# Emitting the first batch's attention steps inside a high-priority scheduling block

## The chip, the cores and the metric

The kernel runs on one core of one Trainium2 chip. The metric is device time in microseconds (us) of one execution; a timing is the median of several executions. The engines are PE (TensorE), DVE (VectorE), ACT (ScalarE), POOL (GpSimd) and SP (SyncE, which here only issues DMAs).

## What the kernel computes

All arithmetic is on float32 data. The inputs q, k, v have shape 8 x 8 x 576 x 64 (batch, heads, sequence, head width), p has 32 rows in place of 576.

```
p_packed = softmax(p k^T / 8) v            # 32 packed rows for each head
attn     = softmax(q p_packed^T / 8) p_packed
x = attn, heads side by side               # 4608 tokens x 512
h = x @ w_in                               # 512 -> 1024
s = h * softmax(h)
ln = (s - mean(s)) / sqrt(var(s) + 1e-6) * g_ln
y = ln @ w_out                             # 1024 -> 512
out = max(y @ w1, y @ w2, y @ w3) @ w_out2 # 512 -> 768 -> 512
```

The MoE weights arrive as float64 words, so w_in, w_out, w1, w2, w3 and w_out2 must be decoded to float32 on the chip before they are used.

## The kernel before

**The first part of the program** is attention plus the first expert block, in token tiles of 128 (36 tiles, `tok_hidden`). The attention of a batch is folded into w_in: the packed values of the batch, `ppT`, are multiplied with the decoded w_in, which gives `Mh` and `Ml` (a high and a low part). A tile's hidden row is then the product of its second-softmax weights `ah`, `al` with `Mh`, `Ml` (line 500, `h`). The second part (line 737 onward) is a Strassen-like product with w1, w2, w3 and the output product (line 984).

**A batch's attention** is a `Packed` object whose pieces are called by letters, each with a group or pair number: K `keys` (transposes of p and k into `pT` and `kT`, lines 312 and 319), S `scores` (line 328, then row maxima L336, L337 on DVE, exponentials L341 on ACT, reciprocals L346 to L349), E `weights` (transposes of the exponentials, L357), V `values` (L368, scaled on ACT at L377, transposed at L383 into `ppT`), M `product` (L395, then `Mh` L247 on ACT and `Ml` L248 on DVE), Q `queries` (transposes of q into `qT`, L412), X `tokens` (L428 on PE; then on DVE transposes L434, maximum L438, subtraction L439, sum L442, L443, reciprocal L444, product L445, transposes back L459; the exponential L440 and the cast to `ah`, L460, on ACT; `al`, L461, on POOL). Lower-case k, v, q are loads: one 576 KB DMA for a group of four heads of k or v (L291, L295), three DMAs of 288 KB together for a pair of heads of q (L304 twice, L307 once).

**Buffers that gate loads**: the two k tiles and the two v tiles of a batch share one tag with two buffers, the four q tiles share a tag with two buffers. A third load waits until a buffer is released by its last reader. The raw words of w_in (eight pieces of 512 KB, L179) have six buffers.

**The decode of w_in** runs beside the first batch's attention. A piece takes one or two ACT instructions (L116, L118), three or four DVE instructions (L121, L124, L127, for every second piece L129) and one or two POOL instructions (L132, or L134 and L135). Pieces are numbered by c = 0 to 3 (128 rows each) with two halves each. M0 needs c = 0 and 1, M1 needs c = 2 and 3. Decoding w_out (L199, L200 with the same helpers) follows.

**Order of the work.** The order on each engine's queue is not written by hand. A scheduler walks the program against modelled durations and gives an idle engine, DMA queue or buffer to the ready instruction with the smallest priority number. The number is the place in the program text: earlier text, smaller number. Waiting for another engine's result is then fixed into the queue: at run time each engine takes its queue in order. The list that orders the first batch is

```
st=['K0S0K1v0q0', '', 'v1', 'q1E0', 'S1V0Q0E1Q1V1M0', 'q2', 'q3Q2Q3X0X1M1', ''],
```

and the loop that emits it stands at the end of the set-up, after the loads of p, k and six pieces of w_in:

```
for i, step in enumerate(CFG['st']):
    first.run(step)
    for d in dec[:2]:
        d()
    dec = dec[2:]
    if i == 0:
        dec += [decode_w_in(NPAIR - 1, n) for n in range(2)]
```

So after each of the first four steps the decode of one c is emitted; the step that begins with S1 comes behind all of the decode in the text. After the loop come the loads of g_ln and w_out, the second batch's attention (`second`, in small steps called between the tiles) and the tiles themselves. Tile 0 needs K, S, E, V, Q, M of both groups and X0; X1 serves tiles 2 and on.

Of the kernel before, what the change touches and what calls it, by code (L numbers as in the profile page):

```python
# [53 lines left out]
def kernel(  # L54
# [127 lines left out]
    def decode_w_in(c, n):  # L182
        ns = slice(n * 512, (n + 1) * 512)
        raw = wide(words(w_in)[c * P:(c + 1) * P, ns, :])
        t = lt_p.tile([P, TB], F32, tag="lh", name="dt")
        t2 = lt_p.tile([P, TB], F32, tag="ll", name="dt2") if CFG['l0'][n] == 'g' else None
        return lambda: [f() for f in decode(w_in_sb[:, c, ns], raw, t, t2, ENG[CFG['d0'][2 * (c % 2) + n]])]
# [616 lines left out]
    first, second = Packed(0), Packed(1)  # L804
# [2 lines left out]
    first.load(1)  # L807
    dec += [decode_w_in(c, n) for c in (1, 2) for n in range(2)]
    for i, step in enumerate(CFG['st']):
        first.run(step)  # L810
        for d in dec[:2]:
            d()
        dec = dec[2:]
        if i == 0:
            dec += [decode_w_in(NPAIR - 1, n) for n in range(2)]
# [268 lines left out]
```

## Time and profile before

| | us |
|---|---|
| median of 3 timed executions | 1119.6 |
| lowest and highest of them | 1118.24 and 1119.76 |
| span of the profiled execution | 1119.7 |
| PE busy in it | 1061.3 (95%) |
| DVE, ACT, POOL busy | 735.0, 483.9, 273.9 |

The time of the profiled execution is its span; no other time of it is recorded, and it lies 0.1 us above the median of the timed runs. A row of the timeline view gives a start time in us from the span's start, a duration, the engine and the source line, the operation with its output and inputs, and in brackets how long the engine sat idle before it and which instruction ended the wait. SPq is the queue of DMA issues; a row of it is the issue, not the transfer. "x6" after a shape counts the instructions that were merged into the row.

### The profile page before, as it was taken

Reading aid. Unit: us, or ns where it says so; the run is one execution under the profiler, and the core shown is the slowest. Engines: PE = TensorE matmul, PEld = TensorE weight load, DVE = VectorE, ACT = ScalarE, POOL = GpSimd, SP = SyncE. Lnnn points to the kernel's source line nnn. Section 1 sums busy time; section 2 is a strip of 40 time slices with the busy share of each in tenths; the row PEclk is TensorE's granted clock in tenths of the full one; section 3 lists DMA queues with packets and bytes.
Section 4 is the critical chain, followed back from the end, with each engine's and each line's share of the span. In section 5 each row is a group of like instructions: output and inputs, shape, how many; then the busy total and the mean of one; then the engine's idle time right before and its main releaser. Section 6 shows DMA issues by size and latency. Waiting matters only on the chain.

```text
span 1119.7 us, 17559 instructions
## 1 busy us (share of the span) xinstructions
PE 1061.3 (95%) x6308; PEld 885.5 (79%) x6308; DVE 735.0 (66%) x1454; ACT 483.9 (43%) x951; POOL 273.9 (24%) x283
## 2 busy tenths in 40 slices
PE   4799999999999999999789999999999999999998
PEld 2456667676767777787678899989989999998996
DVE  5788897968787895766686734745664573572560
ACT  3676766665666666456343321321142131132112
POOL 3442311111112110103576410230041041132002
PEclk9798999999999999999899999999999999999999
DMA  9842636464565622310674533534454353443421
GB/s 260 195 104 58 183 106 178 128 167 125 134 177 139 167 83 63 113 38 19 225 226 141 175 119 121 169 112 133 144 167 132 114 177 117 121 123 104 132 76 57
DMA packets 132262, 149.01 MB, mean 133 GB/s; under 512 B 51536, under 2 KB 85328, under 8 KB 132176
## 3 DMA queue, kind: packets, MB, share of 16 engines
q1 hardware_dynamic: 132176, 147.89, 45.2%
q8 instruction: 50, 0.82, 0.3%
q14 instruction: 36, 0.29, 0.1%
HBM read 113.25 MB, written 34.60 MB: 132 GB/s over the span
## 4 chain that ended last, share of the span: by engine, by line
PE 52%; DVE 4%; issue 3%; POOL 2%; ACT 1%; DMA 1%; SPq 0%; DVEq 0%; POOLq 0%; ACTq 0%
PE m L737 31%; PE o L984 13%; PE y L591 4%; PE h L500 2%; POOL s L640 1%; PE tp L566 1%; DMA wt<-wdram 1%; DVE s L646 1%; DVE v L776 0%; POOL al L640 0%; DVE u L772 0%; PE mp L395 0%; DVE u L510 0%; DVE nm L506 0%; DVE r L759 0%
## 5 line engine op out<-in xcount | busy, mean ns | idle before, releaser
L591 PE MATMUL y<-lh,woh 128*128 128x512 f32 x288 | 118.5, 416 | 0.8 <-ACT lh L572 0.8
L772 DVE TENSOR_TENSOR u<-m,q 128x384 f32<-128x384 f32 x54 | 29.9, 554 | 134.7 <-ACT ob L993 75.7
L591 PE MATMUL y<-ll,woh 128*128 128x512 f32 x288 | 115.8, 402 | 0.0
L591 PE MATMUL y<-lh,wol 128*128 128x512 f32 x288 | 114.6, 398 | 0.0
L768 ACT COPY q<-m 128x384 f32<-128x384 f32 x54 | 25.9, 480 | 168.2 <-PE m L737 168.2
L799 POOL TENSOR_TENSOR hl<-cur,hh 128x384 fp32r<-128x384 f32 x36 | 37.7, 1047 | 243.8 <-ACT hh L798 243.8
L132 POOL TENSOR_TENSOR wt<-raw 128x256 f32<-128x256 f32 x56 | 34.4, 615 | 213.3 <-DVE raw L129 116.9
L984 PE MATMUL o<-w2h,hh 128*128 128x512 f32 x216 | 85.3, 395 | 0.0
L984 PE MATMUL o<-w2h,hl 128*128 128x512 f32 x216 | 85.3, 395 | 0.0
L984 PE MATMUL o<-w2l,hh 128*128 128x512 f32 x216 | 85.3, 395 | 0.0
L737 PE MATMUL m<-b22h,s 128*128 128x384 f32 x216 | 65.7, 344 | 2.3 <-DVE r L759 2.0
L591 PEld LDWEIGHTS y<-lh,woh 128*128 128x128 f32 x288 | 53.9, 189 | 14.2 <-ACT lh L572 1.1
L591 PEld LDWEIGHTS y<-lh,wol 128*128 128x128 f32 x288 | 54.6, 190 | 12.3
L737 PE MATMUL m<-t2h,s 128*128 128x384 f32 x216 | 64.2, 337 | 0.0
L591 PEld LDWEIGHTS y<-ll,woh 128*128 128x128 f32 x288 | 54.7, 190 | 11.7 <-issue 1.0
L737 PE MATMUL m<-t1h,s 128*128 128x384 f32 x216 | 63.7, 335 | 0.1
L737 PE MATMUL m<-t3h,s 128*128 128x384 f32 x216 | 63.5, 334 | 0.0
L798 ACT CAST hh<-cur 128x384 fp32r<-128x384 f32 x36 | 18.5, 514 | 90.4 <-DVE cur L785 49.0
L573 DVE SCALAR_TENSOR_TENSOR ll<-tp,g_sb,lh 128x512 fp32r<-128x512 f32 x72 | 52.0, 744 | 8.1 <-ACT lh L572 7.8
L572 ACT ACTIVATE lh<-tp,g_sb 128x512 fp32r<-128x512 f32 x72 | 47.3, 686 | 22.5 <-PE tp L566 22.4
L799 POOL TENSOR_TENSOR hl<-kept,hh 128x384 fp32r<-128x384 f32 x36 | 38.8, 1077 | 72.5 <-ACT hh L798 72.5
L506 DVE TENSOR_REDUCE nm<-h 128x1 f32<-128x1024 f32 x36 | 43.9, 1219 | 17.8 <-PE h L500 17.5
(189 smaller groups left out, 2912.2 us busy)
## 6 DMA issues: line engine op xcount, KB each, us to landing
s<-sdram SPq DMA_DIRECT2D x180, 256.0 KB, 2.8
kt<-in_k_dram SPq DMA_DIRECT2D x16, 576.0 KB, 5.2
vt<-in_v_dram SPq DMA_DIRECT2D x16, 576.0 KB, 4.8
ydram<-yt SPq DMA_DIRECT2D x36, 256.0 KB, 3.2
raw<-in_moe_w_dram SPq DMA_DIRECT2D x36, 256.0 KB, 2.9
b<-ydram SPq DMA_DIRECT2D x24, 384.0 KB, 3.5
sdram<-s SPq DMA_DIRECT2D x36, 256.0 KB, 2.1
out_dram<-ob SPq DMA_DIRECT2D x36, 256.0 KB, 2.0
```

What stands on the lines that cost most here:

```text
L132: add.tensor_tensor(out=dst, in0=f32(hi), in1=f32(lo), op=ALU.add)
L500: nc.tensor.matmul(h[:, n, :], lhsT=x, rhs=m[:, g, n * 512:(n + 1) * 512], start=(i == 0), stop=(i == len(ops) - 1),)
L506: nc.vector.tensor_reduce(out=nm, in_=hv, axis=AX.X, op=ALU.max, negate=True)
L572: last[nc.scalar] = nc.scalar.activation(lh, tp, AF.Copy, scale=gc)
L573: last[nc.vector] = nc.vector.scalar_tensor_tensor(out=ll, in0=tp, scalar=gc, in1=f32(lh), op0=ALU.mult, op1=ALU.subtract)
L591: nc.tensor.matmul(ys[half][m], lhsT=w[:, kc, ms], rhs=x, start=(kc == 0 and i == 0), stop=(kc == KFF - 1 and i == 2),)
L737: nc.tensor.matmul(out, lhsT=w, rhs=y, start=start and i == 0, stop=i == len(ops) - 1, skip_group_check=not start,)
L768: nc.scalar.copy(q, ba)
L772: add(out=u, in0=bb, in1=q, op=ALU.add)
L798: nc.scalar.copy(hh, t)
L799: nc.gpsimd.tensor_tensor(out=hl, in0=t, in1=f32(hh), op=ALU.subtract)
L984: nc.tensor.matmul(ops[i], lhsT=x[:, ts], rhs=w, start=(c == 0 and n == 0), stop=(c == KF2 - 1 and n == 2),)
```

## The change

The call that emits a step of the first batch's attention is wrapped in the scheduler's high-priority context. By its definition the context, when no offset is given, sets the priority counter to 0, the start of the program, and puts it back on exit. The instructions of each step, its DMA issues among them, are therefore numbered 0, 1, 2, ... anew in each of the eight steps, and everything emitted outside (the decode of w_in, the loads of p, k and w_in, the second batch, the tiles) is numbered as if the steps took no numbers. No instruction is added or removed and no buffer is changed.

```
     for i, step in enumerate(CFG['st']):
-        first.run(step)
+        with tc.high_priority():
+            first.run(step)
         for d in dec[:2]:
             d()
         dec = dec[2:]
```

## Rows read from the trace of the kernel before

**Rows 1.** The page, busy tenths of the span in 40 equal slices.
```profile
PE   4799999999999999999789999999999999999998
```

**Rows 2.** Windows: stretch, its length, busy us (instructions) of each engine, clock, DMA.
```profile
0.00:8.00 8.00, 0.67 (x3) 0.41 (x4) 0.00 (x0) 1.28 (x1) 1.69 (x15) 1.00 0.69 184
8.00:20.00 12.00, 10.15 (x63) 5.47 (x62) 8.57 (x15) 8.71 (x24) 3.67 (x3) 1.00 1.07 308
20.00:30.00 10.00, 0.88 (x48) 0.74 (x48) 8.76 (x18) 2.65 (x9) 5.95 (x5) 0.65 0.85 212
30.00:40.00 10.00, 8.86 (x88) 5.90 (x90) 6.09 (x11) 7.35 (x20) 5.69 (x5) 0.83 0.59 130
40.00:50.00 10.00, 5.95 (x37) 2.93 (x31) 9.12 (x18) 6.07 (x14) 4.02 (x3) 0.85 1.04 254
50.00:60.00 10.00, 9.80 (x46) 6.05 (x47) 6.58 (x13) 4.47 (x11) 3.87 (x3) 0.64 0.68 167
60.00:80.00 20.00, 17.57 (x188) 11.30 (x189) 16.98 (x43) 17.23 (x39) 10.51 (x8) 1.00 0.59 142
80.00:112.00 32.00, 29.90 (x153) 19.80 (x149) 26.08 (x60) 23.08 (x46) 6.44 (x11) 0.89 0.19 51
200.00:400.00 200.00, 197.07 (x1361) 142.91 (x1354) 163.45 (x411) 130.66 (x265) 31.37 (x47) 1.00 0.52 143
```

**Rows 3.** Timeline, all engines, 9 to 32 us.
```profile
9.51 0.43 DVE L121 TENSOR_SCALAR dt<-dt 128x512 int32<-128x512 int32 x1 [9.51 <-ACT dt L116]
...
21.58 0.45 DVE L336 TENSOR_REDUCE m<-s 128x1 f32<-128x288 f32 x1
...
28.19 0.20 DVE L337 TENSOR_SCALAR m<-m 128x1 f32<-128x1 f32 x1
28.49 0.50 ACT L341 ACTIVATE e<-s,m 128x288 f32<-128x288 f32 x1 [7.32 <-DVE m L337]
...
30.03 0.48 PE L383 MATMUL tp<-ident,ppz 128*128 128x128 f32 x1 [7.74 <-ACT ppz L377]
...
31.56 0.67 ACT L116 ACTIVATE dt<-raw 128x512 f32<-128x512 f32 x1
```

**Rows 4.** Timeline of the DMA issue queue, 10 to 36 us.
```profile
10.45 0.33 SPq L295 DMA_DIRECT2D vt<-in_v_dram  x1
10.82 2.80 SPq L304 DMA_DIRECT2D qtl<-in_q_dram  x2
...
31.69 0.92 SPq L304 DMA_DIRECT2D qtl<-in_q_dram  x2
```

**Rows 5.** DMA issues of 1.73 to 2.2 us (KB each, us from issue to landing).
```profile
kt<-in_k_dram SPq DMA_DIRECT2D x1, 576.0 KB, 6.0
```

**Rows 6.** DMA issues of 17.0 to 18.8 us and of 18.85 to 19.6 us.
```profile
raw<-in_moe_w_in_dram SPq DMA_DIRECT2D x1, 512.0 KB, 7.8
vt<-in_v_dram SPq DMA_DIRECT2D x1, 576.0 KB, 9.1
```

**Rows 7.** Timeline, all engines, 33 to 62 us.
```profile
33.85 0.88 PE L368 MATMUL pv<-vt,e1T 96*32 96x64 f32 x48
...
36.20 0.27 ACT L242 COPY ppT<-tp 128x128 f32<-128x128 f32 x1 [0.42 <-PE tp L383]
...
38.53 1.30 POOL L135 TENSOR_TENSOR w_in_sb<-raw,dt 128x512 f32<-128x512 f32 x1
...
39.59 2.16 PE L428 MATMUL st<-qT,ppT 128*64 128x256 f32 x16
...
41.58 1.89 PE L395 MATMUL mp<-w_in_sb,ppT 128*64 128x512 f32 x8
...
49.55 0.60 ACT L460 CAST ahsmall<-y 128x512 fp32r<-128x512 f32 x1
...
50.20 0.79 PE L500 MATMUL h<-Mh,ahsmall 128*128 128x512 f32 x1 [1.55 <-ACT ahsmall L460]
...
60.69 0.90 DVE L459 STREAM_TRANSPOSE y<-x 128x320 f32<-128x320 f32 x2
```

More of the change, by code (lines that the diff above doesn't have):

```diff
@@ L809 @@
     for i, step in enumerate(CFG['st']):
-        first.run(step)
+        with tc.high_priority():
+            first.run(step)
         for d in dec[:2]:
```

## The prediction

> **What bounds the kernel now.** I first read where PE is idle, since it is busy for 95% of the span. The slices of the page [rows 1] show the reader two thin places at the start and nearly full slices behind them but for a dip in the second half that this change does not touch. The windows [rows 2] give sizes: up to 60 us PE is busy 0.67 + 10.15 + 0.88 + 8.86 + 5.95 + 9.80 = 36.31 us, so idle for 23.7; from 60 to 112 it is idle for 4.5; from 200 to 400 it is 98.5% busy. What reaches PE earlier at the start therefore stays earlier to the end, and the start is where this change acts.
>
> In the start PE is not the limit; DVE is, and behind it the loads. DVE is busy for 39.12 us of the first 60 [rows 2]. Its idle time is 8.0 (0 to 8), 3.4 (8 to 20), 1.2 (20 to 30), 3.9 (30 to 40), 0.9 (40 to 50) and 3.4 (50 to 60). The first three are waits for loads at the beginning. The last three, 8.2 us together, come from one chain. DVE ends the second row maximum of S1 at 22.0, but the 0.20 us instruction that joins the two maxima stands behind decode work in the queue and runs only at 28.19; ACT waited 7.32 us for it, PE 7.74 us for what ACT does next [rows 3]. The next q load waits too: q2 is issued at 31.69 [rows 4] and q3 behind it, so X's products begin only at 39.59, and its cast on ACT ends at 49.55 + 0.60 = 50.15, when tile 0 starts at 50.20 [rows 7]. The last piece of w_in has the same fate: its words were issued by 18.8 and landed 7.8 us later [rows 6], near 26, but the decode of c = 3 begins on ACT at 31.56, behind the delayed exponentials [rows 3], and ends at 39.83 on POOL [rows 7].
>
> **The change, part by part.** *No work is added or taken away.* Instruction counts and sizes stay, so the whole sum is waits and order.
>
> *Attention before decode on DVE, ACT and PE.* The S1 step gets numbers from 0 instead of numbers behind all decode, so its small DVE instructions pass the decode. The decode of w_in is numbered from about 17 to 70 (seven instructions of set-up, ten loads, then 13 instructions for each c; counted in the text), and those of S1 (0 to 15) lie below all of it, those of X0 (17 to 35) below c = 2 and 3 and most of c = 1. V1 (66 and on) and M0 (94 and on) do not pass it. M0 also loses its place against the second batch's first transposes (81 to 98), which are short; I cost that at nothing, as PE has 23.7 us of room, and at the 2.2 us by which a run can be told from no change if that room is gone. What is to be had is the 8.2 us of DVE idle time in 30 to 60 us. The bounds are 0, if new waits replace the old, and 8.2 + 3.1 = 11.3, if the waits of 8 to 30 us (4.6, less the 1.5 us from 8 to DVE's first instruction at 9.51 [rows 3]) go as well. I take 8.2: those early waits are for loads, and the loads become no faster.
>
> *Loads.* Every DMA issue inside a step moves too. v1, q1, q2 and q3 are the first items of their steps, so they are numbered 0 to 2, ahead of p (7) and k0 (9). A free buffer goes to the smallest number that is ready; at the start all are free. So v1 takes one of the two k/v buffers, q1 and q2 the two q buffers, and all seven issues go out before p. That puts 576 + 2 x 288 = 1152 KB ahead of the first load that anything waits for. The price: between the landing of k0 (issued 1.74, 6.0 us, so 7.7) [rows 5] and that of v1 (18.91 + 9.1 = 28.0) [rows 6], 6112 KB came down: the eight pieces of w_in (4096 KB), k1, v0 and v1 (1728) and q0 (288). That is 301 KB per us, a full pipe, since both windows in it show DMA shares of 1.07 and 0.85 [rows 2]. So the moved loads cost 1152 / 301 = 3.8 us at the start of everything. The bounds are 0 (buffers given out in the order of the text after all) and 6.3 (the 184 GB/s of the first window [rows 2]); I take 3.8, from the full pipe.
>
> k1 loses its buffer to v1. It waits until K0 has read k0, then v0 waits for K1. I follow the bytes: k0 lands at 11.5; then c = 0, 1 and 2 (3072 KB), k1 (576), q3 (288), c = 3 (1024), q0 (288) and v0 (576), 5824 KB or 19.3 us, so v0 lands at 30.8. From the start of V on PE to ppT took 36.47 - 33.85 = 2.6 us; from X's products to the cast 50.15 - 39.59 = 10.6 us [rows 7]. Tile 0 could so start at 30.8 + 2.6 + 10.6 = 44.0 instead of 50.2. This chain thus leaves room for more than the DVE count does, and the smaller gain rules: DVE begins 3.8 us later and saves 8.2 us of waits, a net 4.4 us.
>
> *Sum.* 1119.7 (the profiled execution's span) - 8.2 + 3.8 = 1115.3 us. The median of the runs, 1119.6, is 0.1 below that execution, less than I can resolve.
>
> One rule speaks against the moved q loads. Their rows are 256 bytes. The windows of 8 to 20 us, with q0's load queued, still ran at 308 GB/s [rows 2], so no row shows a price for that. The Trainium skill, DMA: Bandwidth & Descriptors, Specifications, asks for at least 512 bytes in a transfer for line rate, since below that a DMA engine reads, modifies and writes; no run here shows it by itself, and what it would make of the sum stands among the rivals.
>
> **The rivals.**
>
> *Loads held in the issue queue: slower.* SP issues in order, and an issue that waits for a buffer holds all behind it. In the trace of before, q0 had a free buffer from the start and was issued only at 10.82, behind v0, which waited for K0 until 10.45 [rows 4]. With small numbers, k1 and q3 may be put ahead of the pieces c = 1 and 2, and stop them until K0 or Q1 is done. Such a hole is at least K0's time, from 7.7 (k0's landing) to 10.45, 2.7 us [rows 4, 5]; when the pipe runs dry behind it, it takes a load's 6.0 us [rows 5] more, 8.7. With a full hole the time is 1119.7 + 3.8 + 8.7 - 8.2 = 1124.0. It decides once the holes come to more than 8.2 - 3.8 + 2.2 = 6.6 us. Against it: the pieces already queued keep the pipe busy for about 3.4 us for c = 0 alone (1024 KB). For it: the scheduler's model does not know this pipe's load, as the wait for q0 shows.
>
> *X1 ahead of the last decode: no change.* X1's numbers (36 and on) also lie below those of c = 3 (58 to 70). If DVE takes X1 before c = 3, that decode begins after two chains like X0's, and M1, whose products began at 41.58 [rows 7], comes later than before by about what X1, whose last transposes ended at 61.6 [rows 7], comes earlier. What DVE gains is spent on work that tile 0 doesn't need: the 4.4 us are lost to PE's wait for M1, and the time stays at 1119.7. For it speaks the numbering; against it that c = 3 lands at 28 by the count above, before X0 can start at 33.4.
>
> *Buffers given out in the order of the text: faster still.* The change then moves only the work on the engines, the 3.8 us are not paid, and the time is 1119.7 - 8.2 = 1111.5. Against it: the description of the scheduler says that any ready instruction takes a free buffer.
>
> *Slow q rows: hardly faster.* If q1 and q2 come at half the rate, their 576 KB take 3.8 us instead of 1.9, and the time is 1117.2. For it speaks only the rule of the Trainium skill named above; the 308 GB/s with q0 in the pipe speak against it.
>
> **How the numbers follow.** A run of this kernel can be told from no change at about 0.2%, 2.2 us. I give the forecast 0.35, text-order buffers 0.13, slow q rows 0.07, X1 ahead 0.18 and the held queue 0.27. The first three are faster: 0.55; X1 ahead is the same: 0.18; the held queue is slower: 0.27. The predicted time is the likeliest case, 1115.3. Its own range is 1111.5 to 1117.5 (from no hoist to the point of no change). The range over the cases reaches from 1109.0, which is 1111.5 with most of the 3.1 us of early waits gone, to 1124.0, the full hole.
>
> **What would show it.** Right: the first issues on the DMA queue are v and q loads and p lands 3 to 5 us later; DVE's first decode instruction starts near 13 us instead of 9.5; ACT no longer waits 7 us for the joined maximum of S1; X's products begin by 34 and tile 0 by 46; DVE idle between 30 and 60 us is below 3. Wrong: if p is still first, the buffers follow the text; if SP shows waits of several us ahead of w_in pieces, the queue was held; if c = 3 is decoded behind X1, M1 is what tile 0 waits for. The prediction also fails if the shift at 60 us is given back by 200, for instance because the second batch's work, now behind, holds up tiles 4 and on.

## The result, and the profile after

The changed kernel takes 1126.7 us (median of 4, 1123.93 to 1128.47) against 1119.68 for the kernel before (4, 1118.24 to 1120.62). The ratio is 1.006 with a 95% interval of 1.0042 to 1.0078: 0.6% slower, where 1115.3 was forecast and 1124.0 was the upper end. The span of the profiled execution grew from 1119.7 to 1125.5. That execution itself took 1127.31, 1.8 more than its span, and the same 1.8 lie between time and span in most runs below. The execution behind the rows of before thus took an estimated 1121.5, not the 1119.7 that the prediction's sum started from. Medians give the sizes below; traces give the places.

The page's slices of PE answer to [rows 1]: only the second and the third differ.

```profile
PE   4889999999999999999789999999999999999998
```

The windows answer to [rows 2], with the same columns.

```profile
20.00:30.00 10.00, 2.42 (x51) 1.94 (x52) 10.00 (x18) 4.09 (x11) 5.95 (x4) 0.52 0.96 187
30.00:40.00 10.00, 9.31 (x73) 5.02 (x72) 7.20 (x9) 5.05 (x12) 7.04 (x7) 0.50 0.59 155
40.00:50.00 10.00, 8.35 (x46) 3.93 (x44) 5.96 (x12) 5.14 (x13) 1.92 (x2) 0.95 0.87 218
50.00:60.00 10.00, 8.43 (x34) 4.99 (x35) 6.50 (x13) 4.87 (x10) 3.24 (x3) 0.56 0.74 170
...
200.00:400.00 200.00, 197.37 (x1398) 144.47 (x1397) 162.85 (x410) 130.43 (x263) 31.24 (x47) 1.00 0.53 146
```

From 200 to 400 us hardly anything has changed. In the start PE's clock is at half from 20 to 40 us and again in most of 50 to 60, and DVE is idle for 2.8 + 4.0 + 3.5 = 10.3 us of 30 to 60, more than before, not less.

The DMA issue queue, to be held against [rows 4], shows the first surprise.

```profile
0.74 0.95 SPq L285 DMA_DIRECT2D p_sb<-in_p_dram  x2
1.74 0.46 SPq L291 DMA_DIRECT2D kt<-in_k_dram  x1
2.24 0.95 SPq L179 DMA_DIRECT2D raw<-in_moe_w_in_dram  x2
3.23 0.43 SPq L291 DMA_DIRECT2D kt<-in_k_dram  x1
3.71 13.29 SPq L179 DMA_DIRECT2D raw<-in_moe_w_in_dram  x6
17.05 0.95 SPq L295 DMA_DIRECT2D vt<-in_v_dram  x2
18.04 2.16 SPq L304 DMA_DIRECT2D qtl<-in_q_dram  x3
20.24 3.88 SPq L307 DMA_DIRECT2D qtl<-in_q_dram  x1
...
26.89 1.72 SPq L825 DMA_DIRECT2D raw<-in_moe_w_out_dram  x1
31.19 3.30 SPq L304 DMA_DIRECT2D qtl<-in_q_dram  x4
```

The order up to k1 is that of before, so v1, q1 and q2 did not go out ahead of p. But six pieces of w_in follow instead of four: the two of c = 3 now stand ahead of v0 and q0. Their buffers are those of the first two pieces, and until the decode has read these, SP waits. v0 goes out at 17.05 instead of 10.45. Behind it v1 and q1 are mixed with q0, and q2 and q3 come behind the first load of w_out.

The timeline of all engines answers to [rows 3, 7].

```profile
20.50 0.20 DVE L337 TENSOR_SCALAR m<-m 128x1 f32<-128x1 f32 x1
20.80 0.50 ACT L341 ACTIVATE e<-s,m 128x288 f32<-128x288 f32 x1 [1.38 <-DVE m L337]
...
24.16 1.51 PE L368 MATMUL pv<-vt,e1T 96*32 96x64 f32 x48 [6.27 <-DMA vt<-in_v_dram]
...
29.57 1.08 PE L412 MATMUL tp<-ident,qtl 128*128 128x128 f32 x4 [2.79 <-DMA qtl<-in_q_dram]
...
36.07 3.68 PE L395 MATMUL mp<-w_in_sb,ppT 128*64 128x512 f32 x6
...
40.68 0.62 ACT L199 CAST woh<-wt 128x512 fp32r<-128x512 f32 x1 [1.97 <-POOL wt L135]
...
42.97 2.16 PE L428 MATMUL st<-qT,ppT 128*64 128x256 f32 x16
44.96 1.89 PE L395 MATMUL mp<-w_in_sb,ppT 128*64 128x512 f32 x8
...
52.04 0.80 PE L500 MATMUL h<-Mh,ahsmall 128*128 128x512 f32 x1 [1.55 <-ACT ahsmall L460]
```

The forecast's mechanism is there: the join of S1 runs 7.7 us earlier (20.50 for 28.19) and ACT waits 1.38 us for it, not 7.32. But PE now waits 6.27 us for v0 and 2.79 us for q0, then runs at half clock. X's products begin 3.4 us later than before (42.97 for 39.59) and tile 0 1.8 us later (52.04 for 50.20). By the row maxima of the tiles (L506) the shift against before is 2.8 us at tile 0 (61.24 for 58.48) and 7.3 at tile 2 (79.37 for 72.12). It varies to tile 5 and then stays between 4.0 and 5.0 to tile 35. The two spans differ by 5.8 us and the medians by 7.0, so a part arises behind these tiles, and the execution behind the rows of before was a rather slow one.

### The profile page after: what moved, and what is told of

Same layout as the page of the kernel before. It is cut to its first block, busy times and chain, and to the rows that moved or that the text cites. A ratio compares the mean times of both kernels' runs of the same rounds, so it can differ in the third digit from the quotient of the medians.

```text
span 1125.5 us, 17554 instructions
## 1 busy us (share of the span) xinstructions
PE 1068.1 (95%) x6308; PEld 889.4 (79%) x6308; DVE 742.3 (66%) x1454; ACT 484.2 (43%) x951; POOL 274.8 (24%) x283
## 4 chain that ended last, share of the span: by engine, by line
PE 52%; DVE 4%; issue 3%; POOL 2%; DMA 1%; ACT 1%; SPq 0%; DVEq 0%; POOLq 0%; ACTq 0%
PE m L737 31%; PE o L985 13%; PE y L591 4%; PE h L500 2%; POOL s L640 1%; PE tp L566 1%; DVE s L646 1%; DMA wt<-wdram 1%; DVE v L776 0%; POOL al L640 0%; DVE u L772 0%; PE mp L395 0%; DVE u L510 0%; DVE nm L506 0%; DVE r L759 0%
## 5 line engine op out<-in xcount | busy, mean ns | idle before, releaser
L506 DVE TENSOR_REDUCE nm<-h 128x1 f32<-128x1024 f32 x36 | 43.8, 1217 | 19.7 <-PE h L500 19.4
L760 DVE TENSOR_TENSOR kept<-r,kept 128x384 f32<-128x384 f32 x72 | 55.2, 767 | 2.0
L508 ACT ACTIVATE u<-h,nm 128x1024 f32<-128x1024 f32 x36 | 40.2, 1117 | 36.5 <-DVE nm L506 36.2
```

The costliest lines, as they stand in the source:

```text
L506: nc.vector.tensor_reduce(out=nm, in_=hv, axis=AX.X, op=ALU.max, negate=True)
L508: nc.scalar.activation(u, hv, AF.Exp, bias=nm, accum_out=sums[:, t:t + 1])
L760: add(out=cur[m, n], in0=r, in1=cur[m, n], op=ALU.max)
```

## The experiments

Each ratio is to runs of the kernel before on the same chip (medians 1118.8 to 1119.5), with its 95% interval. The first theories were: (A) the held queue alone costs it, as v0 comes late; (B) the smaller numbers of everything outside the steps cost it; (C) attention ahead of decode costs it by itself.

**keep_numbers.** Against the change: the numbers that a step used are added back, so everything outside the steps is numbered as before.

```
+        start = tc.cur_priority
         with tc.high_priority():
             first.run(step)
+            count = tc.cur_priority
+        tc.cur_priority = start + count
```

> The steps are numbered from 0 as in the change, but after each step the counter goes on behind the numbers that the step used, so the rest of the program (decode of w_in with its loads, w_out, second batch, tiles) is numbered as in the kernel before. The last two pieces of w_in then stand behind v0 and q0 in the issue queue. Theory A (the queue: these two pieces, numbered 47 and 48, got ahead of v0 with 52 and held the queue until 17.0 us): v0 is issued near 10.5 us and the 7 us are gone, ratio to the kernel before 0.998 to 1.000. Theory B (the rest of the program, with numbers some 100 to 190 smaller, passes M0, X and the second batch's work on ACT and DVE): gone as well, 0.998 to 1.001. Theory C (attention ahead of the decode is itself what costs): still 1.004 to 1.006.

Measured: 1117.04, ratio 0.9984 [0.9973, 0.9995]. C falls: with all steps raised the kernel is a little faster. Its queue has four pieces of w_in and then v0:

```profile
3.70 2.05 SPq L179 DMA_DIRECT2D raw<-in_moe_w_in_dram  x4
9.53 5.99 SPq L295 DMA_DIRECT2D vt<-in_v_dram  x2
...
21.66 1.06 SPq L179 DMA_DIRECT2D raw<-in_moe_w_in_dram  x2
```

**loads_outside.** Against the change: the v and q loads of each step are emitted ahead of it, outside the block.

```
+        loads = ''.join(step[n:n + 2] for n in range(0, len(step), 2) if step[n] in 'vq')
+        first.run(loads)
         with tc.high_priority():
-            first.run(step)
+            first.run(''.join(step[n:n + 2] for n in range(0, len(step), 2) if step[n] not in 'vq'))
```

> The change, but the loads of v and q in a step are emitted ahead of it and outside the high-priority block, so v0 and q0 have smaller numbers than the last pieces of w_in; the rest of the program is still numbered as if the steps' arithmetic took no numbers. Theory A (the queue): v0 is issued near 10.5 us and the loss is gone, ratio 0.998 to 1.001. Theory B (smaller numbers of the rest): 1.003 to 1.006, with the w_out decode still ahead of X's copies on ACT. Theory C (attention ahead of the decode): 1.004 to 1.006.

Measured: 1118.16, ratio 0.9991 [0.9979, 1.0002]. The decode and the rest keep their smaller numbers here and nothing is lost. B falls; the loss comes through the loads.

**s1_only.** Against before: only S1 is raised, with the numbers behind it given back.

```
+        if step.startswith('S1'):
+            start = tc.cur_priority
+            with tc.high_priority():
+                first.run('S1')
+                count = tc.cur_priority
+            tc.cur_priority = start + count
+            first.run(step[2:])
+        else:
+            first.run(step)
```

> Of all steps only S1, the scores of the second group, is put into the high-priority block, and the rest keeps its numbers; the issue queue's order is that of the kernel before. The forecast's own mechanism alone: ACT's wait of 7.3 us for the joined maximum goes. If that wait was what the start waits for (the forecast): X's products begin by 36 us and the ratio is 0.995 to 0.998. If what lies behind it (q2 and q3, the last decode) is late for a reason of its own (loads): X's products begin within 1 us of 39.6 and the ratio is 0.999 to 1.001. Theory C: above 1.002.

Measured: 1117.28, ratio 0.9985 [0.9976, 0.9994]. This is the forecast's mechanism alone, 1.7 us rather than 8.2. The join runs at 20.55, but PE then waits for q1:

```profile
28.84 1.38 PE L412 MATMUL tp<-ident,qtl 128*128 128x128 f32 x5 [2.27 <-DMA qtl<-in_q_dram]
...
38.41 1.89 PE L428 MATMUL st<-qT,ppT 128*64 128x256 f32 x14
```

**c3_first.** Against before: the two pieces of c = 3 are emitted ahead of v0; no step is raised.

```
-        first.run(step)
+        if i == 0:
+            first.run(step[:6])
+            last_c = [decode_w_in(NPAIR - 1, n) for n in range(2)]
+            first.run(step[6:])
...
-            dec += [decode_w_in(NPAIR - 1, n) for n in range(2)]
+            dec += last_c
```

> The kernel before, without any high priority, with one edit in the text: the two loads of the last pieces of w_in are emitted between K1 and v0 instead of behind the step, which puts them ahead of v0 and q0 in the issue queue as in the changed kernel. Theory A: v0 is issued near 17 us, and most of the loss is there without any priority, ratio 1.003 to 1.006. Theory B or C: 0.999 to 1.001.

Measured: 1129.33, ratio 1.0087 [1.0071, 1.0102]. It has the loss, but not for A's reason alone: on DVE the decode of c = 3 also got ahead of S1's join, which ran at 32.94, and ACT waited 10.25 us for it. So the two were parted:

**c3_first_s1.** c3_first, with S1 raised as in s1_only.

```
+        elif step.startswith('S1'):
+            start = tc.cur_priority
+            with tc.high_priority():
+                first.run('S1')
...
```

> The kernel before with the last pieces of w_in ahead of v0 and q0 in the issue queue, and with S1 alone in the high-priority block, the rest keeping its numbers. In the run with only the pieces moved, the loss of 8 to 9 us came with two things: v0 held until 17 us, and the decode of c = 3 ahead of S1's joined maximum on DVE (32.9 instead of 28.2 us). Here the second is gone. If holding the queue costs by itself: V0 still starts near 24 us and the ratio is 1.002 to 1.005. If the loss was the decode ahead of S1: 0.998 to 1.000.

Measured: 1118.68, ratio 0.9996 [0.9984, 1.0008]. A falls. The queue is held as in the change and v0 is as late, yet nothing is lost against before (against s1_only's 0.9985 it may be 1 us; the intervals overlap):

```profile
3.70 13.55 SPq L179 DMA_DIRECT2D raw<-in_moe_w_in_dram  x6
17.31 0.42 SPq L295 DMA_DIRECT2D vt<-in_v_dram  x1
17.78 1.23 SPq L304 DMA_DIRECT2D qtl<-in_q_dram  x2
19.05 0.72 SPq L307 DMA_DIRECT2D qtl<-in_q_dram  x1
19.88 0.52 SPq L295 DMA_DIRECT2D vt<-in_v_dram  x1
```

```profile
24.32 1.51 PE L368 MATMUL pv<-vt,e1T 96*32 96x64 f32 x48 [6.57 <-DMA vt<-in_v_dram]
...
26.72 1.36 PE L412 MATMUL tp<-ident,qtl 128*128 128x128 f32 x5
```

All of q0 goes out ahead of v1 here, and Q0 follows V0 without a wait, at 26.72. In the change v1 stands ahead of q0, q1 between its parts, and Q0 runs at 29.57.

**pool_issue.** Against the change: the two loads of c = 3 are issued from POOL's queue.

```
-        raw = wide(words(w_in)[c * P:(c + 1) * P, ns, :])
+        raw = wide(words(w_in)[c * P:(c + 1) * P, ns, :], nc.gpsimd if c == NPAIR - 1 else nc.sync)
```

> The change with one edit: the loads of the last two pieces of w_in are issued from POOL's queue, so nothing that waits for a w_in buffer stands ahead of v0 in SP's queue; the order on PE, DVE and ACT is that of the changed kernel. If the held queue costs the time: v0 is issued near 10 us, V0 starts near 20 us, ratio to the kernel before 0.997 to 1.001. If the order on PE, DVE and ACT that the change brought costs it by itself: 1.003 to 1.006 although v0 comes early.

Measured: 1126.93, ratio 1.007 [1.0058, 1.0083]. It doesn't decide, since it made a new wait. v0 went out at 9.57, but ACT's queue held the decode of c = 3 ahead of V0's scaling, so the scaling waited, twice for some 2 us, for loads that POOL issued at 16.69; and w_out's first load still went out ahead of q2 (22.09):

```profile
24.59 0.66 ACT L116 ACTIVATE dt<-raw 128x512 f32<-128x512 f32 x1 [2.05 <-DMA raw<-in_moe_w_in_dram]
...
28.52 0.51 ACT L377 ACTIVATE ppz<-pv,rim 128x64 f32<-128x64 f32 x2
```

**one_run.** Against the change: the steps share one run of small numbers instead of each beginning at 0, and the rest stays behind them.

```
+    steps_end = tc.cur_priority
+    tc.cur_priority += 400
...
         with tc.high_priority():
+            tc.cur_priority = steps_end
             first.run(step)
+            steps_end = tc.cur_priority
```

> All steps of the first batch are numbered in one run, one behind the other, and everything else of the program behind all of them; the forecast's picture of attention ahead of the decode, without numbers that start anew and without pieces of w_in ahead of v0. The issue queue then takes v and q of the batch before the last pieces of w_in, which wait behind q3. If attention is what the start waits for: tile 0 starts by 47 us, ratio 0.995 to 0.998. If the decode of c = 3 is then late: M1 is what tile 0 waits for, ratio 0.999 to 1.004.

Measured: 1120.78, ratio 1.0018 [1.0008, 1.0027]. X's products begin early, at 32.92, but the decode of c = 3 is late: M1 waits for it on POOL (2.56 us at 39.35, 1.23 us at 45.86) and tile 0 starts at 47.76. Attention wholly first costs M1, as one of the rivals had it; the changed kernel shows no such wait.

**change_again.** The change, unedited, beside these.

> The changed kernel once more, on the same chip as the three others, so that they can be compared with it: ratio to the kernel before 1.004 to 1.007, v0 issued near 17 us, V0 starting near 24 us.

Measured: 1126.85, ratio 1.0072 [1.006, 1.0084].

The theory then was (D): it takes both, c = 3 ahead of v0 and v1, q1 ahead of the rest of q0. Three runs tried it.

**first_loads_outside** and **later_loads_outside.** Against the change: the loads of step 0 (v0, q0), or those of the later steps (v1, q1, q2, q3), are emitted outside the block.

```
+        loads = 'vq' if i == 0 else ''        # first_loads_outside
+        later = 'vq' if i else ''             # later_loads_outside
```

> The change, but v0 and q0 are emitted ahead of the first step and outside the block, so their numbers lie below those of the last two pieces of w_in; v1 and q1 still get ahead of most of q0. Theory D in its full form (it takes both, the held queue and v1 and q1 ahead of q0): v0 is issued near 10 us, Q0 starts before 26 us, ratio 0.997 to 1.000. If v1 and q1 ahead of q0 cost by themselves: 1.002 to 1.005.

> The change, but the loads v1, q1, q2 and q3 are emitted ahead of their step and outside the high-priority block, so v1 and q1 no longer get ahead of q0; the last two pieces of w_in still stand ahead of v0 in the issue queue and hold it until 17 us. Theory D (the held queue alone is covered, but v1 and q1 between v0 and the rest of q0 make q0 land 3 us later, and the second group's transposes, V1 and M0 stand behind Q0 on PE): v0 as late as in the change, Q0 before 27.5 instead of 29.6 us, ratio 0.998 to 1.001. Theory A (the held queue costs by itself): 1.003 to 1.006.

Measured: 1117.59, ratio 0.9981 [0.997, 0.9993], and 1118.65, ratio 0.999 [0.9977, 1.0003]. In the second c = 3 is still ahead of v0 (issued at 17.48, V0 at 24.57), but Q0 runs at 26.98. Removing either half removes the whole loss, as D says. But both edits move a third thing: w_out's first load goes out behind q2 and q3 again (at 32.04 and 33.50), where the change has it ahead of them (26.89). So they do not part the place of v1 and q1 from the place of that load.

**v1_q1_first.** c3_first_s1, with v1 and q1's loads emitted where the change's queue has them; only S1 is raised.

```
-            first.run(step[6:])
+            first.run('v0v1q0')
...
+                if self.b == 0 and c == 0 and hh == 0:
+                    self.load_q(1)
```

> The kernel with the last two pieces of w_in ahead of v0 and S1 alone in the high-priority block (0.9996 before), and in addition v1 and q1 emitted behind the first third of q0's loads, so that SP's queue has the order of the changed kernel down to the second load of w_out, and nothing else has a raised priority. Theory D: Q0 starts near 29.5 us, X's products begin near 42 us, ratio 1.003 to 1.007. If the order of these loads is not the cause: 0.999 to 1.001.

Measured: 1120.39, ratio 1.0011 [1.0001, 1.0022]. The queue is the change's, and V0 (23.93) and Q0 (29.95) run as late, yet only some 1.2 us are lost, where 1.003 to 1.007 was expected. This order of loads does not make the loss: most of it has to come from what the other raised steps do with late data.

**c3_early_keep.** keep_numbers, but the two loads of c = 3 are numbered 47 and 48 as in the change, ahead of v0 (52).

```
+            start = tc.cur_priority
+            tc.cur_priority = 46
             dec += [decode_w_in(NPAIR - 1, n) for n in range(2)]
+            count = tc.cur_priority - 46
+            tc.cur_priority = start + count
```

> All steps raised, every number behind each step given back as before (the kernel that gained 0.16%), but the two loads of c=3 numbered 47 and 48, ahead of v0 and q0. If the place of those two loads is all that the rewinding did, the time is the change's again, about 1126.5 (ratio 1.006 to 1.008, c=3 issued at 3.7 and held until 17). If the smaller numbers of w_in's decode have a part in the loss, it comes out lower, 1119 to 1123.

Measured: 1125.93, ratio 1.0059 [1.0047, 1.0072]: the change's time again. Beside keep_numbers' 0.9984 the place of two load issues accounts for all of the loss; the other smaller numbers outside the steps are not needed for it.

**up_to_m0** and **up_to_e0.** Against the change: only the steps up to the one that ends with M0, or up to E0, are raised.

```
-        with tc.high_priority():
-            first.run(step)
+        if i < 5:                             # up_to_e0: i < 4
+            with tc.high_priority():
+                first.run(step)
+        else:
+            first.run(step)
```

> The change with the steps q2 and q3 Q2 Q3 X0 X1 M1 left at their own numbers. Loads of c=3 still ahead of v0, v1 and q1 ahead of the rest of q0. If the loss arises before M0 (q0 late, E1 and V1 behind it), it stays: ratio 1.006 to 1.008, tiles 6 on later by 4 to 5 us. If it arises in the raised last steps (M0's fourth product behind Q2, ScalarE's copies in another order), it falls to about 1.001, tiles later by 0 to 2 us.

> The change with S1 V0 Q0 E1 Q1 V1 M0 left at their own numbers as well: only the first loads, K, S0, v1, q1 and E0 are raised. If the raised E0 and the early loads alone cost it, ratio 1.006 or more, and S1's join on DVE is late again (28 us or more). If the raised S1 to M0, together with the late q0, cost it, ratio about 1.001 to 1.003.

Measured: 1121.05, ratio 1.0017 [1.0008, 1.0026], and 1124.73, ratio 1.0047 [1.0033, 1.006]. up_to_e0 is slow for the old reason (the join runs at 32.78). up_to_m0 is the clean pair to the change: X's products begin at 43.00 (42.97 in the change), M1's at 44.99 (44.96), tile 0's at 51.73 (52.04), and still its maxima (L506) lead the change's by 2.5 us at tile 0, 2.6 at tile 1 and 4.8 from tile 2 to tile 5. Rows of up_to_m0, tile 0's maximum among them:

```profile
57.20 0.69 DVE L443 TENSOR_SCALAR sm<-sm 128x20 f32<-128x20 f32 x1
...
58.78 1.22 DVE L506 TENSOR_REDUCE nm<-h 128x1 f32<-128x1024 f32 x1 [0.88 <-PE h L500]
...
63.73 0.73 ACT L460 CAST ahlarge<-y 128x640 fp32r<-128x640 f32 x1 [1.06 <-DVE y L459]
...
65.00 1.01 PE L357 MATMUL tp<-ident,e 128*96 128x128 f32 x6 [1.99 <-ACT e L341]
```

The change has these rows instead.

```profile
61.24 1.22 DVE L506 TENSOR_REDUCE nm<-h 128x1 f32<-128x1024 f32 x1 [2.56 <-PE h L500]
...
62.38 1.25 DVE L443 TENSOR_SCALAR sm<-sm 128x20 f32<-128x20 f32 x1
...
67.46 0.72 ACT L460 CAST ahlarge<-y 128x640 fp32r<-128x640 f32 x1 [1.80 <-DVE nmu L512]
...
68.73 1.51 PE L357 MATMUL tp<-ident,e 128*96 128x128 f32 x6 [3.37 <-ACT e L341]
```

The windows of 2 us say where. First up_to_m0, then the change.

```profile
56.00:58.00 2.00, 2.00 (x7) 1.58 (x7) 1.90 (x5) 0.21 (x1) 1.34 (x2) 0.67 1.09 294
58.00:60.00 2.00, 2.00 (x16) 1.51 (x15) 1.22 (x2) 1.08 (x3) 1.25 (x1) 1.00 0.13 22
```

```profile
58.00:60.00 2.00, 2.00 (x6) 1.60 (x5) 0.67 (x1) 0.00 (x0) 1.92 (x2) 0.50 0.15 27
60.00:62.00 2.00, 2.00 (x11) 1.51 (x11) 0.76 (x1) 0.55 (x2) 0.62 (x1) 0.64 0.00 0
...
68.00:70.00 2.00, 1.27 (x6) 1.19 (x7) 2.00 (x2) 2.00 (x6) 1.55 (x1) 0.56 0.00 0
```

In up_to_m0 the clock is full again from 58 us on and stays so to 80. In the change it is at half until about 61, so tile 0's products, begun only 0.3 us later, end 2.5 us later. The order on DVE differs too. A small instruction of X1 (L443) stands ahead of tile 0's maximum (L506) in up_to_m0, at 57.20; in the change it stands behind it, at 62.38, and so waits for tile 0's products. X1's cast on ACT comes 3.7 us later (67.46 for 63.73). The second batch's exponentials stand behind that cast, so PE sits idle for 3.37 us to 68.73 in the change and for 1.99 us to 65.00 in up_to_m0. The clock falls a second time in the change only: its six transposes of e take 1.51 us, not 1.01. From them to the next scores (L328) PE takes 6.95 us in the change (68.73 to 75.68) and 6.08 in up_to_m0 (65.00 to 71.08).

The sizes of these stretches are not fixed. In the trace of change_again, the same kernel, the clock is back at about 59 and tile 0's maximum is only 1.3 us behind that of up_to_m0, yet from tile 4 on the shift is again about 5 us. What recurs is the order: L443 behind L506 and a wait of PE of some 3.4 us. It stands so in the traces of all four runs at 1.006 to 1.007 with every step raised (the change twice, pool_issue, c3_early_keep). one_run has that order too, but tile 0's maximum comes at 52.83 there and PE waits only 1.45 us.

**w_out_later.** Against the change: w_out's first load is emitted behind the second batch's first loads.

```
-    for _ in range(CFG['pre']):
-        load_w_out()
     second.load(0)
     second.load(1)
+    for _ in range(CFG['pre']):
+        load_w_out()
```

> The change with the first load of w_out emitted behind the second batch's first loads, so that neither its load stands ahead of q2 and q3 on SP nor its copy (line 199, which waited 1.97 us for POOL) ahead of the copies of q on ScalarE. If that copy and that load cost X its 2 to 3 us, st begins before 41 and the ratio is 1.003 to 1.005; if they only fill a wait for M0's products, st stays at about 43 and the ratio at 1.006 to 1.008.

Measured: 1120.52, ratio 1.0014 [1.0006, 1.0023]. All steps raised and c = 3 ahead of v0 (issued at 17.47), but X's products begin at 39.65, M0's eight take 1.94 us, and tile 0's maximum comes at 56.57, right behind X1's L443:

```profile
36.01 1.94 PE L395 MATMUL mp<-w_in_sb,ppT 128*64 128x512 f32 x8
...
39.65 0.65 PE L428 MATMUL st<-qT,ppT 128*64 128x256 f32 x2
...
56.49 0.17 DVE L443 TENSOR_SCALAR sm<-sm 128x20 f32<-128x20 f32 x1
56.57 1.22 DVE L506 TENSOR_REDUCE nm<-h 128x1 f32<-128x1024 f32 x1
```

So moving w_out's first load back behind q2 and q3 (to 37.80), and its decode with it, is a second way to take most of the loss out, a larger part than was expected (1.003 to 1.005). PE idles even longer before the second batch's transposes here (3.74 us to 63.95) and its clock falls too (0.50 from 66 to 70 us); still, from tile 4 on the maxima are up to 1.3 us ahead of before's. keep_numbers, faster than before, shows such a second fall as well (0.50 from 64 to 68 us). So that wait and that fall by themselves do not make the loss.

## Why the prediction was wrong, point by point

*Attention before decode* was right as a mechanism and wrong as a size. The join's delay went, as forecast. But the 8.2 us were DVE's idle time, read as what PE would get back. Alone (s1_only) it is worth 1.7 us, and with all steps raised under before's loads (keep_numbers) 2.0, because other waits stand close behind. In s1_only the next one is the wait for q1, which ends at 28.84. DVE's idle time of 30 to 60 us did not shrink to below 3; it is 6.0 in keep_numbers.

*Loads* is the step that failed, and the one that decided the sign. The prediction has v1, q1, q2 and q3 out ahead of p for 3.8 us. They were not: p and k0 are issued when they were. That fits buffers of one tag going out in the order of the text, as the rival "Buffers given out in the order of the text" has it; no run tested this by itself. The rival's time, 1111.5, fails with the 8.2. What the prediction missed is what the change does to loads outside the steps. v0 and q0 come at the end of their step and keep numbers of about 50, while the pieces of c = 3, emitted after the step, no longer count its numbers and come below them (47 and 48, as they were counted for the runs). They pass v0 and hold SP for their buffers until 17. The prediction's count of bytes did have c = 3 ahead of q0 and v0, but it charged only the bytes and not the wait for buffers. In place of the 3.8 us the runs show the step from keep_numbers (0.9984) to c3_early_keep (1.0059): an estimated 8.4 us for the place of two load issues. With a gain of 1.8 us in place of 8.2 that makes 6.6 us, beside the 7.0 measured.

The path from v0 to tile 0 was wrong as well. v0 was forecast to land at 30.8, with X's products 2.6 us behind it. PE had v0 at 24.16, and X's products began 18.8 us later: Q0, E1, Q1, V1 and M0 stand between them on PE, most of it at half clock.

*k1 loses its buffer to v1* did not happen; k1 is issued at 3.23, ahead of c = 1.

*Loads held in the issue queue*, given 0.27, came nearest: the sign, an issue that waits for a buffer, and 1124.0 for 1126.7. But its place differs (c = 3 ahead of v0, not k1 or q3 ahead of c = 1 and 2), and so does its price, and its sum holds the 3.8 and the 8.2 that were not there, so the near number is luck. The hold by itself costs nothing that the runs can show (c3_first_s1, 0.9996). With v1 and q1 mixed into q0, so that Q0 is 3 us later, and w_out's load ahead of q2, it costs about 1.2 us (v1_q1_first). *X1 ahead of the last decode* shows in one_run and not in the change. *Slow q rows* were not put to the test.

The loss thus needs several things together. One edit each shows that it needs c = 3 ahead of v0 (c3_early_keep has it, keep_numbers does not), the later steps raised (up_to_m0, 1.0017) and w_out's first load ahead of q2 (w_out_later, 1.0014). That it also needs v1 and q1 ahead of the rest of q0 is not shown: later_loads_outside, which takes the loss out, moves w_out's load as well. In the pair of up_to_m0 and the change the traces put 4.8 us of the difference into the two stretches described, tile 0's products at half clock and the second batch's wait and half clock before tile 2.

What stays open: why PE's clock returns at 58 us in one order and at 61 in another though PE was busy from 52 on in both, and at 59 in a second trace of the changed kernel. That the clock is the cause of the first 2.2 us is read from the windows; no run changed the clock alone. Nor did a run change only the order of X1's small instruction and tile 0's maximum on DVE, so what that order costs is argued from the traces and not shown.

## What to carry to other kernels

When a scheduler's numbers are changed, work out the new numbers of what is not raised too: a counter that is put back pulls everything behind it forward, and the damage here began with two load issues that passed another load and waited for a buffer. Time that one engine waits is an upper bound for what removing the wait can give; before it is entered in a sum, look for what arrives next on the engine that sets the end (here q1; 8.2 us of wait became 1.7 us of time). And when removing any one of several parts removes a loss, look for the combination, with one run for each part alone, and check in its trace that nothing else moved.

## What the runs showed of the hardware

A DVE instruction of one kind (128x512, tensor with scalar, int32) takes 0.42 us or over three times as long, by what POOL does at that moment. The changed kernel's timeline of DVE and of POOL:

```profile
21.22 0.42 DVE L121 TENSOR_SCALAR dt<-dt 128x512 int32<-128x512 int32 x1
22.12 1.59 POOL L134 TENSOR_TENSOR dt<-dt,dt 128x512 f32<-128x512 f32 x1 [2.62 <-DVE dt L127]
22.62 1.38 DVE L127 TENSOR_SCALAR dt<-raw 128x512 int32<-128x512 int32 x1
```

So DVE's busy time holds waiting: it is "busy" for all of 20 to 30 us with 18 instructions, as many as before in 8.76 us [rows 2]. The Trainium skill, SBUF — State Buffer, Who interferes with whom, says that these two engines share a port pair as an exclusive lock: where a DVE instruction takes that pair, whichever engine comes second waits for the whole of the other's instruction. The rows agree: the long one begins inside the POOL instruction, which ends at 23.71, and ends 0.29 us after it.

PE's clock is at one of two levels here, half (1.2 GHz) or full (2.4 GHz), and V's 48 products took 1.51 us at the one and 0.88 at the other. In the changed kernel it fell again at 68 us, after PE had been idle for 3.37 us; in up_to_m0 the 1.99 us of idleness there were followed by no fall, in w_out_later the 3.74 us were. The Trainium skill, TensorE: Matmul & The Clock Gate, HAM oscillation, has the same picture: waits for data send PE back to half clock, and the next work pays for it. The clock column is not to be read alone, though. In up_to_m0 it shows 1.00 for 20 to 40 us, while V1's 48 products took 1.51 us and six of M0's 3.59, as in the changed kernel at half clock. For the two stretches above the durations were read beside it: a product of tile 0 takes 0.63 us to 61 in the changed kernel, and 0.40 from 57.4 in up_to_m0.
